# One projection for queries, keys and values in a four-layer attention kernel, and reworked joints between its layers

## The chip, the cores and the metric

The kernel runs on one core of one Trainium2 chip, as one program. The metric is the device time of an execution in microseconds (us). Three runs of the kernel before took 2574.44, 2575.98 and 2577.28 us; their median is 2575.98.

## The reference

Four layers follow one another on a residual of 2048 tokens by 640 features: A, B, A, B. Both A layers share their weights, and so do both B layers.

```
x = A_x
x = x + _A_ref(_layernorm(x), A_wq, A_wk, A_wv, A_wo, A_beta)
x = x + _B_ref(_layernorm(x), B_mem0, B_Wq, B_Wk, B_Wv, B_Wo, B_seg_len)
x = x + _A_ref(_layernorm(x), ...)
x = x + _B_ref(_layernorm(x), ...)
```

Layer A has 32 heads of 20 features and cuts the tokens into 4 segments of 512. In each segment it computes a causal softmax attention within the segment, and reads a memory that the earlier segments have written:

```
q, k, v = x @ wq, x @ wk, x @ wv                  # per head, per segment
a_dot = softmax(q k^T / sqrt(20) + causal mask) v
a_mem = phi(q) M / (phi(q) z + 1e-6)              # phi(t) = t + 1 where t > 0, else exp(t)
o     = g * a_mem + (1 - g) * a_dot               # g = sigmoid(beta), one a head
M, z  = M + phi(k)^T v, z + sum of phi(k)         # after the segment
```

Layer B has 32 heads of 128 features and is recurrent: 64 steps of 32 tokens, each with 8 memory tokens in front that come out of the step before. Its first 8 outputs are the next step's memory.

## The kernel before, in words

**Engines' order.** The tensor engine's instructions (PE) are issued in the order of the program text. In layer A the other engines are ordered by `KeyOrder`: an operation is noted with a due time, the time of its slot (`K.base`) plus a lag by its kind from the table `A_LAGS`, and each engine runs its operations in order of due time. In layer B all engines follow the program text (`_OrdNC`). DMAs are issued from SP's queue.

**Layer A.** `layer_A` works on 32 groups: 4 segments (n) by 8 groups of four heads (G), g = 8n + G. Four heads of 20 features are padded to 32 each and fill 128 rows. A group has four slots, numbered 4g to 4g + 3. In each slot PE first makes "visits": score tiles S (`s_mask` puts the causal mask into PSUM with a whole-array matmul, `s_mm` adds q k^T on 32-row tiles, VectorE takes the row maximum into `a_nm`) and turned tiles T of the group before (`t_round`, exponential on ScalarE into `a_PT`, diagonal cut by GpSimd). After the visits `filler` runs the slot's items, listed in `SLOTS`:

- QP (`proj_q`): the next group's queries, already turned (features on rows, 512 tokens on columns), five matmuls 512 wide; ScalarE copies them to `a_qT`. From the second segment on phi(q) is made from it (`a_EQ`, `a_rq`, `a_phiq`).
- KV0, KV1 (`proj_kv`): keys and values in natural layout (tokens on rows), ten matmuls 160 wide each; ScalarE copies keys to `a_Kn` and values to `a_vaug`, padded to 32 a head.
- KT (`k_turn`): four transposes of the keys and a copy to `a_kT`.
- Q2 (`q_with_max`): the queries go once more through PE with an identity, and the negated row maximum (written by `negmax_rows` in two bf16 parts into columns 20 and 21 of the tile `a_NM`) is turned and added into the same PSUM tile; the copy is `a_q2`, which the T tiles use, so that their scores come out with the maximum taken off.
- UP (`state_up`): phi(k)^T v of the group before, four 128x128 matmuls; VectorE masks the block diagonal (`a_upm`), GpSimd adds it to the state `MZ32` and casts it to `MZb`.
- NUM (`state_num`), PV (`pv`, `norm`), otps, YP0 and YP1 (`out_stage_a`, `out_stage_b`): the memory's read, the attention's output, and the output projection of the segment before with the residual.

The items' PSUM tiles share a pool of two banks (`pg`), so an item waits until the copy of the tile two before it is done. S and T tiles share three tiles of two banks (`psx`). The next segment's layernorm and turn (`seg_load`, `seg_norm`, `seg_tr`) stand in the slots of groups 0 to 4 of a segment (`TPS`).

**Joints.** At the start of a layer A four x tiles are loaded, normalised (`seg_norm`) and turned (`seg_tr`), with idle matmuls (`unread`) between. The first A layer loads plain weights and casts them into padded tiles `a_wq_pad` and `a_wkv` (`load_A_weights`); `keep_padded` stores these to DRAM, and the second A layer loads them from there on SP's queue. `build_gates` makes g and 1 - g after the first visits. At the end of a layer A `out_stage_b` runs for four token tiles: it loads the residual (`a_xr`) for the last two only when it reaches them, and casts each result to bf16 on ScalarE in one single buffer (`a_xnb`) before it is stored; layer B loads that again for its own layernorm.

**Layer B's last step.** Each of the 64 steps projects the next step's tokens (`thin_mm`: b_Ka, b_Qa, b_Kb, b_Qb, 20 matmuls each on four 32-column tiles), where only the 8 memory columns come from the step before. The last step has no next tokens, so its columns (`HXz`) hold the memory alone, and its queries are those of the memory tokens, whose outputs nobody reads. Outputs for the last 8 tokens of four steps are gathered in `OTdef` and projected in four chunks (`od_chunk`, `od_begin`, `od_end`) within later steps; for the last four steps this stands after the last step.

Of the kernel before, what the change touches and what calls it, by code (L numbers as in the profile page):

```python
# [28 lines left out]
D = 640  # L29
NCH = 5  # L30
# [7 lines left out]
def alloc_consts(tc, ctx):  # L38
# [7 lines left out]
    C.pad = cp.tile([128, 2, 12], BF16, name="c_pad")  # L46
# [10 lines left out]
def build_consts(nc, tc, C):  # L57
    with ExitStack() as tctx:
# [13 lines left out]
        for i in range(2):  # L72
            nc.vector.tensor_copy(C.negu[:, i, :], neguf[:])
# [125 lines left out]
class AWeights:  # L199
# [3 lines left out]
A_LAGS = {"dsel": 0.5, "EK": -1.0, "EKm": 1.05, "EQ": 2.0, "Kn": 0.5, "MZ": 3.5, "MZb": 3.5, "NM1": -0.3, "On": 3.2, "adn":  # L203
# [6 lines left out]
def build_gates(nc, pool, W, A_beta):  # L210
    bb = pool.tile([128, 32], BF16, name="a_beta_bf")
    with nc.allow_non_contiguous_dma(reason="beta bcast"):
        nc.sync.dma_start(bb[:], A_beta.partition_broadcast(128))
    e = pool.tile([128, 32], F32, name="a_beta_e")
# [9 lines left out]
def load_A_weights(nc, W, A_wq, A_wk, A_wv, A_wo, padded, stage):  # L224

    first = not padded
    if first:
        for nm, src in (("wq", A_wq), ("wk", A_wk), ("wv", A_wv)):
            nc.sync.dma_start(stage[nm], src.rearrange("(c p) n -> p c n", p=128))
    else:  # L230
        nc.sync.dma_start(W.wq[:].rearrange("p c h s -> p (c h s)"), padded["wq"])
        nc.sync.dma_start(W.wkv[:].rearrange("p c g n -> p (c g n)"), padded["wkv"])
    nc.sync.dma_start(W.wo[:], A_wo.rearrange("(c p) n -> p c n", p=128))
    if first:
        K = yield
        nc.gpsimd.memset(W.wq[:, :, :, 20:32], 0.0)
        cast = K("cast").vector
        cast.tensor_copy(W.wq[:, :, :, 0:20], stage["wq"].rearrange("p c (h d) -> p c h d", d=20))
        for i, nm in enumerate(("wk", "wv")):
            cast.tensor_copy(W.wkv[:, :, :, 80 * i:80 * i + 80], stage[nm].rearrange("p c (g n) -> p c g n", n=80))  # L240
        yield


def keep_padded(nc, tc, W, padded):
    for nm, pad, n in (("wq", W.wq, 1024), ("wkv", W.wkv, 1280)):
        padded[nm] = tc.dram_tile([128, NCH * n], BF16, name=f"a_{nm}_home")
        nc.sync.dma_start(padded[nm], pad[:].rearrange("p c h s -> p (c h s)"))


def layer_A(nc, tc, C, W, x_src, x_dst, src_is_bf16, nseg=4, out_bf16=False, xb_dst=None, load_w=None, side_loads=None):  # L250
# [7 lines left out]
    with ExitStack() as ctx:  # L258
# [4 lines left out]
        W.wq = pw.tile([128, NCH, 32, 32], BF16, name="a_wq_pad")  # L263
        W.wkv = pw.tile([128, NCH, 8, 160], BF16, name="a_wkv")
# [6 lines left out]
        qp3 = pool("a_q3", 3)  # L271
# [18 lines left out]
        MZ32 = ste.tile([128, 8, 128], F32, name="a_MZ32")  # L290
        nc.vector.memset(MZ32[:], 0.0)
        MZb = stm.tile([128, 8, 128], BF16, name="a_MZb")
        vaug = [stm.tile([128, 4, 4, 32], BF16, name=f"a_vaug{i}") for i in range(4)]
        Kn = [stm.tile([128, 4, 4, 32], BF16, name=f"a_Kn{i}") for i in range(2)]
        phik = [ste.tile([128, 4, 4, 32], BF16, name=f"a_phik{i}") for i in range(2)]
        NM = [stm.tile([128, 4, 4, 32], BF16, name=f"a_NM{i}") for i in range(2)]

        def pads(i, eng):
            for on, dst, k in ((i < 2, Kn, 0), (True, vaug, 1)):
                if on:  # L300
                    src = C.pad[:, k, :].unsqueeze(1).unsqueeze(1).to_broadcast([128, 4, 4, 12])
                    (eng.copy if eng is nc.scalar else eng.tensor_copy)(dst[i][:, :, :, 20:32], src)

        nc.vector.tensor_scalar(out=MZ32[:].rearrange("p g (j e) -> p g j e", e=32)[:, :, :, 20],
                                in0=C.identb[:].rearrange("p (j e) -> p j e", e=32)[:, :, 20].unsqueeze(1).to_broadcast([128, 8, 4]),
                                scalar1=1e-6, scalar2=None, op0=ALU.mult)
# [20 lines left out]
        def seg_norm(n_, tt):  # L327
# [4 lines left out]
            for i in range(2):  # L332
                K("st").vector.bn_stats(out=stats[:, i, :], in_=xt[:, 320 * i:320 * i + 320])
# [31 lines left out]
        def out_stage_b(n_, tt, halves=(0, 1)):  # L365
# [3 lines left out]
            if xr is None:  # L369
                xr = wkl.tile([128, D], BF16 if src_is_bf16 else F32, name="a_xr")  # L370
                nc.sync.dma_start(xr[:], x_src[r0:r0 + 128, :])
# [14 lines left out]
            xnb = w1l.tile([128, D], BF16, name="a_xnb")  # L386
            if n_ == nseg - 1:
                nc.scalar.copy(xnb[:], xnew[:])
            else:
                K("xnb").gpsimd.tensor_copy(xnb[:], xnew[:])  # L390
            nc.sync.dma_start(xb_dst[r0:r0 + 128, :], xnb[:])
# [3 lines left out]
        def proj_q(g):  # L395
            n, G = divmod(g, 8)
            s_ = GS[g] = {}
            xnT = SEG[n]["xnT"]
            wqG = W.wq[:, :, 4 * G:4 * G + 4, :].rearrange("p c h s -> p c (h s)")
            QP = pg.tile([128, 512], F32, name="a_QP", tag="pg")  # L400
            for c in range(NCH):
                nc.tensor.matmul(QP[:], lhsT=wqG[:, c, :], rhs=xnT[:, c, :], start=(c == 0), stop=(c == NCH - 1))
            qT = qp3.tile([128, 512], BF16, name="a_qT")
            K("qT").scalar.copy(qT[:], QP[:])
            s_["qT"] = qT
            if n >= 1:
                EQ = w1.tile([128, 512], BF16, name="a_EQ")
                K("EQ").scalar.activation(out=EQ[:], in_=qT[:], func=ACT.Exp)
                rq = w1.tile([128, 512], BF16, name="a_rq")
                K("rq").vector.tensor_scalar(out=rq[:], in0=qT[:], scalar1=0.0, scalar2=None, op0=ALU.max)  # L410
# [3 lines left out]

        def proj_kv(g, hf):
# [973 lines left out]
```

## Time and profile before

| what | us |
|---|---|
| median of three runs | 2575.98 |
| the profiled execution's own time | 2574.74 |
| its span (first to last instruction) | 2573.0 |
| PE busy in the span | 2486.0 |
| DVE (VectorE) busy | 1675.5 |
| ACT (ScalarE) busy | 1519.1 |
| POOL (GpSimd) busy | 696.2 |
| row maxima of A (DVE, 512 instructions) | 395.0 |
| exponentials of A (ACT, 384) | 345.8 |
| k and v projections of A (PE, 1280 matmuls) | 111.2 |
| q projections of A (PE, 320) | 79.9 |
| state updates of A (PE, 192) | 18.6 |

A time is a group's busy time, with overlaps counted once. PE's matmuls overlap in the pipeline, so a mean duration is longer than what one more matmul costs. The profile's page also divides the span into 40 slices of 64.3 us and gives each engine's busy share in tenths; layer A is in slices 1 to 5 and 20 to 25. The chain of waits is followed back from the last instruction: a piece is what the end waited for at that time. In rows of chosen stretches the columns are: length, then busy time (and count) of PE, weight loads (PEld), DVE, ACT and POOL, PE's granted clock, the DMA engines' busy share and GB/s.

### The profile page before, as it was taken

The page shows a single profiled execution, that of the slowest core. Times are in us where ns is not written, and L with a number is a line of the kernel's source. Part 1 is how long each engine was busy: PE and PEld are TensorE (multiplying, and loading weights), DVE is VectorE, ACT ScalarE, POOL GpSimd, SP SyncE. Part 2 cuts the span into 40 slices and gives each one's busy share as a digit, 9 for nine tenths or more (in the row PEclk, how much of TensorE's full clock was granted, in tenths as well). Part 3 has the DMA queues.
Part 4 walks back from the last instruction along what each step waited for, and adds up shares of the span by engine and source line. Part 5 has one row for each costly group of instructions (what it writes and reads, how often), then busy time and mean ns, then how long its engine had stood idle before and what let it go on. Part 6 is the DMA issues. An engine that isn't in the chain of part 4 may idle for free.

```text
span 2573.0 us, 139432 instructions
## 1 busy us (share of the span) xinstructions
PE 2486.0 (97%) x62088; PEld 1639.1 (64%) x62088; DVE 1675.5 (65%) x4597; ACT 1519.1 (59%) x3430; POOL 696.2 (27%) x1471
## 2 busy tenths in 40 slices
PE   7999999999999999999989999999999999999998
PEld 5666576666666666666655665766666666666665
DVE  8999845565556556555579998455655655555555
ACT  6999945555555545444369999445554555555443
POOL 5677621111111111111146776111111111111110
PEclk9999999999999999999999999999999999999999
DMA  4122372222222222121220212721212122111111
GB/s 158 46 85 78 91 239 45 50 48 44 51 45 48 46 50 46 39 39 29 63 84 17 68 53 86 233 47 43 45 41 50 42 45 47 42 42 34 38 26 21
DMA packets 325308, 157.18 MB, mean 61 GB/s; under 512 B 244960, under 2 KB 309600, under 8 KB 322912
## 3 DMA queue, kind: packets, MB, share of 16 engines
q1 hardware_dynamic: 324704, 148.26, 22.1%
q8 instruction: 485, 7.95, 1.3%
q14 instruction: 119, 0.97, 0.1%
HBM read 96.46 MB, written 51.71 MB: 58 GB/s over the span
## 4 chain that ended last, share of the span: by engine, by line
PE 78%; DVE 10%; ACT 8%; issue 2%; DMA 1%; POOL 1%; SPq 0%; ACTq 0%; DVEq 0%; POOLq 0%
PE b_OPS L110 11%; PE b_tail L110 6%; PE b_Ka L110 5%; PE b_Kb L110 5%; PE b_Qa L110 5%; PE b_Qb L110 5%; PE b_Va L110 5%; PE b_Vb L110 4%; DVE a_nm L139 4%; PE b_SP L110 4%; ACT a_PT L139 4%; PE b_vtail L110 3%; PE b_OPSd L110 3%; PE b_OTP L110 3%; PE a_S L110 2%
## 5 line engine op out<-in xcount | busy, mean ns | idle before, releaser
L110 PEld LDWEIGHTS <-b_HX 128*32 128x32 bf16 x15360 | 427.8, 96 | 331.3 <-issue 1.3
L110 POOL TENSOR_TENSOR b_Pn<-b_E,b_rs 128x200 bf16<-128x200 bf16 x128 | 78.0, 609 | 1332.7 <-PE b_Vb L110 1016.9
L139 DVE TENSOR_REDUCE a_nm<-a_S 128x2 f32<-128x512 f32 (+3 forms) x512 | 395.0, 816 | 53.1 <-PE a_S L110 38.1
L139 ACT ACTIVATE a_PT<-a_T 128x1024 bf16<-128x1024 f32 (+1 forms) x384 | 345.8, 904 | 28.3 <-PE a_T L110 21.0
L110 PE MATMUL b_OPS<-b_wo,b_OTsb 128*32 128x320 bf16 x8192 | 303.1, 300 | 1.6 <-issue 0.5
L110 PEld LDWEIGHTS <-b_OTsb 128*32 128x32 bf16 x8192 | 205.7, 96 | 76.3 <-DVE b_OTsb L110 3.3
L139 POOL TENSOR_SCALAR_AFFINE_SELECT a_PT<-a_PT 128x256 bf16<-128x256 bf16 x380 | 188.5, 501 | 154.7 <-ACT a_PT L139 153.4
L110 DVE CAST b_HX<-b_MT 128x8 bf16<-128x8 f32 x372 | 63.6, 172 | 234.0 <-PE b_MT L110 228.3
L110 ACT CAST b_msb<-b_OPS 128x64 bf16<-128x64 f32 x378 | 69.5, 256 | 223.7 <-PE b_OPS L110 223.6
L110 ACT CAST b_kq<-b_Kb 128x512 bf16<-128x512 f32 x128 | 74.9, 585 | 201.4 <-PE b_Kb L110 201.4
L110 DVE COPY b_KT<-b_TPak 128x128 bf16<-128x128 bf16 x128 | 28.7, 224 | 228.2 <-PE b_TPak L110 228.2
L110 DVE TENSOR_SCALAR b_kq<-b_Qa 128x512 bf16<-128x512 f32 x128 | 88.5, 691 | 120.1 <-PE b_Qa L110 116.8
L110 PE MATMUL b_Va<-b_wv,b_HX 128*32 128x512 bf16 x2520 | 161.0, 380 | 0.0
L110 PEld LDWEIGHTS <-b_kq 128*128 128x128 bf16 x2080 | 116.8, 98 | 69.4 <-ACT b_kq L110 56.4
L110 PE MATMUL b_Vb<-b_wv,b_HX 128*32 128x512 bf16 x2520 | 160.7, 379 | 0.0
L110 PE MATMUL b_Ka<-b_wk,b_HX 128*32 128x512 bf16 x2520 | 159.1, 379 | 0.1
L110 PE MATMUL b_Qb<-b_wq,b_HX 128*32 128x512 bf16 x2520 | 158.6, 379 | 0.0
L110 PE MATMUL b_Kb<-b_wk,b_HX 128*32 128x512 bf16 x2520 | 158.6, 379 | 0.0
L110 PE MATMUL b_Qa<-b_wq,b_HX 128*32 128x512 bf16 x2520 | 158.6, 379 | 0.0
L110 DVE CAST b_OTsb<-b_OTP 128x160 bf16<-128x160 f32 (+1 forms) x384 | 130.5, 376 | 38.8 <-PE b_OTP L110 34.6
L110 ACT CAST b_kq<-b_Ka 128x512 bf16<-128x512 f32 x128 | 74.9, 585 | 108.9 <-PE b_Ka L110 108.9
L110 PE MATMUL b_vtail<-b_wv,b_TX 128*32 128x256 bf16 x2880 | 133.9, 271 | 2.4 <-issue 2.3
(206 smaller groups left out, 5432.5 us busy)
## 6 DMA issues: line engine op xcount, KB each, us to landing
b_QKd<-b_tu SPq DMA_DIRECT2D x128, 128.0 KB
b_tl<-b_QKd SPq DMA_DIRECT2D x64, 256.0 KB
b_wv<-in_B_Wv_dram SPq DMA_DIRECT2D x10, 1024.0 KB
b_wo<-in_B_Wo_dram SPq DMA_DIRECT2D x16, 640.0 KB
b_Vth<-b_VTd SPq DMA_DIRECT2D x512, 16.0 KB
b_XO<-xres SPq DMA_DIRECT2D x256, 30.0 KB
b_VTd<-b_vt SPq DMA_DIRECT2D x224, 32.0 KB
b_xt<-xres_bf SPq DMA_DIRECT2D x40, 160.0 KB
```

The lines of the kernel that those rows point to most:

```text
L110: r = f(*a, **k)
L139: r = f(*a, **k)
```

## The change

In layer A the queries are projected with keys and values: one weight tile `W.wqkv` of 240 columns a group (80 of q, 80 of k, 80 of v), two halves of ten matmuls (`proj_qkv`), one copy each into a common tile `QKV` with 12 heads of 32 columns, of which `Qn`, `Kn` and `vaug` are views. `qk_turn` turns keys and queries with eight transposes into one PSUM tile, with one copy. Instead of a second pass with added maxima, `negmax_rows` writes the two parts into columns 20 and 21 of the natural queries, and `q_with_max` turns these once more. The state update runs on four 32-column tiles and takes the block diagonal alone; VectorE adds it to a narrower state and GpSimd spreads and masks it to `MZb`. GpSimd's clamp in `phi_k` works on k itself.

At the joints: constants before the first layernorm, norms and turns interleaved, gates loaded first and made before the first projection; the second A layer's weights come in two pieces, on SP's and ScalarE's queues; the residual tiles of the last segment are loaded with the first turns; the last bf16 copies have a place each. The last step of B leaves out its queries' projections (24 columns of its queries come from the step before, the rest is set to zero), projects its own last 8 tokens in its own output matmuls, and does the remaining chunks before PV; the last stores are split between two queues.

```diff
-A_LAGS = {... "EQ": 2.0, "MZ": 3.5, "phiq": 3.6, "rq": 1.1, ...}
+A_LAGS = {... "EQ": 1.3, "MZ": -0.1, "phiq": 2.1, "rq": 1.2, "q0": 0.0, ...}
...
-        nc.sync.dma_start(W.wq[:].rearrange("p c h s -> p (c h s)"), padded["wq"])
-        nc.sync.dma_start(W.wkv[:].rearrange("p c g n -> p (c g n)"), padded["wkv"])
+        home = padded["wqkv"].rearrange("p (c g n) -> p c g n", c=NCH, g=8)
+        nc.sync.dma_start(W.wqkv[:, :, 0:2, :], home[:, :, 0:2, :])
+        f = nc.scalar.dma_start(W.wqkv[:, :, 2:8, :], home[:, :, 2:8, :])
+        tc.add_manual_dep(f.ins, C.act_last.name, ..., reason="order")
...
-        def proj_q(g):
-            QP = pg.tile([128, 512], F32, name="a_QP", tag="pg")
-            for c in range(NCH):
-                nc.tensor.matmul(QP[:], lhsT=wqG[:, c, :], rhs=xnT[:, c, :], ...)
-            K("qT").scalar.copy(qT[:], QP[:])
+        def proj_qkv(g, hf):
+            if hf == 0 and g >= 4:
+                K("q0").gpsimd.memset(Qn[g % 4][:, :, :, 20:22], 0.0)
+            P_ = pg.tile([128, 2, 240], F32, name="a_QKVp", tag="pg")
+            for t2 in range(2):
+                tt = 2 * hf + t2
+                for c in range(NCH):
+                    nc.tensor.matmul(P_[:, t2, :], lhsT=xnT[:, c, 128 * tt:128 * tt + 128], rhs=W.wqkv[:, c, G, :], ...)
+            K("Kn").scalar.copy(QKV[g % 4][:, 2 * hf:2 * hf + 2, :, 0:20], P_[:]...)
+        def qk_turn(g):
+            T_ = pg.tile([128, 2, 4, 128], BF16, name="a_KQT", tag="pg")
+            for i, src in enumerate((Kn[g % 4], Qn[g % 4])):
+                for tt in range(4):
+                    nc.tensor.transpose(T_[:, i, tt, :], src[:, tt, :, :]..., C.identb[:])
+            K("kT").scalar.copy(kq[:]..., T_[:]...)
...
-                UP = pg.tile([128, 128], F32, name="a_UP", tag="pg")
+                UP = pg.tile([128, 32], F32, name="a_UP", tag="pg")
-                    nc.tensor.matmul(UP[:], lhsT=pk[:, tt, :, :]..., rhs=va[:, tt, :, :]..., ...)
-                K("upm").vector.tensor_tensor(out=upm[:], in0=UP[:], in1=C.bdmask[:], op=ALU.mult)
-                K("MZ").gpsimd.tensor_tensor(out=MZ32[:, G, :], in0=MZ32[:, G, :], in1=upm[:], op=ALU.add)
-                K("MZb").gpsimd.tensor_copy(MZb[:, G, :], MZ32[:, G, :])
+                    for j in range(4):
+                        nc.tensor.matmul(UP[32 * j:32 * j + 32, :], lhsT=pk[:, tt, j, :], rhs=va[:, tt, j, :],
+                                         ..., tile_position=(0, 32 * j), skip_group_check=True)
+                K("MZ").vector.tensor_tensor(out=MZ32[:, G, :], in0=UP[:], in1=MZ32[:, G, :], op=ALU.add)
+                K("MZb").gpsimd.tensor_tensor(out=MZb[:, G, :]..., in0=MZ32[:, G, :]...to_broadcast([128, 4, 32]), in1=C.bdmask[:]..., op=ALU.mult)
...
-            Q2 = pg.tile([128, 512], F32, name="a_Q2", tag="pg")
-            nc.tensor.matmul(Q2[:], lhsT=C.identb[:], rhs=s_["qT"][:], start=True, stop=False, ...)
-            for qc in range(4):
-                nc.tensor.matmul(Q2[:, 128 * qc:128 * qc + 128], lhsT=N_[:, qc, :, :]..., rhs=C.identb[:], ...)
+            Q2 = pg.tile([128, 4, 128], BF16, name="a_Q2", tag="pg")
+            for tt in range(4):
+                nc.tensor.transpose(Q2[:, tt, :], Qn[g % 4][:, tt, :, :]..., C.identb[:])
...
-            K.base = 0.1 * tt - 100.0
+            K.base = 1.2 * tt - 100.0
...
-        SLOTS = (('otps', 'QP', 'UP'), ('Q2', 'KV0', 'NUM'), ('KV1', 'YP0'), ('KT', 'PV', 'YP1'))
+        SLOTS = (('otps', 'QKV0', 'UP'), ('Q2', 'QKV1', 'NUM'), ('KQT', 'YP0'), ('PV', 'YP1'))
...
-                    xr = wkl.tile([128, D], ..., name="a_xr") if tt < 2 else None
+                    xr = wkl.tile([128, D], dt_, name="a_xr") if tt < 2 else wk.tile([128, D], dt_, name="a_xr2", tag="a_no")
...
-            xnb = w1l.tile([128, D], BF16, name="a_xnb")
+                if tt == 0:
+                    d["xnb"] = pon.tile([128, 4, D], BF16, name="a_Onat", tag="Onat")
+                xnb = d["xnb"][:, tt, :]
...
+            if last:
+                nc.gpsimd.memset(QT[s][:, :, 24:32], 0.0)
+            else:
+                Qa = thin_mm(cols, W.wq, 0, "b_Qa")
+                qa = kq(Qa, "dve", SCB)
...
+            if last:
+                od_chunk()
+                oda = dict(od)
+                od_begin(s - 3, XOe, "tail")
+                for _ in range(4):
+                    od_chunk()
...
+            if last:
+                od_end(oda)
+                od_end(nm="e")
...
-        for _ in range(4):
-            od_chunk()
-        od_end()
+        C.act_last = nc._prox["scalar"]._last
```

More of the change, by code (lines that the diff above doesn't have):

```diff
@@ L262, in layer_A @@
         pw = pool("a_w", 1)
[L263 to L264 removed]
+        W.wqkv = pw.tile([128, NCH, 8, 240], BF16, name="a_wqkv")
         pxT = pool("a_xnT", 2)
@@ L609, in norm @@
                 K("On").gpsimd.tensor_tensor(out=Ov, in0=s_["AD"][:, 0], in1=AD[:, 1], op=ALU.add)
+        gates = build_gates(nc, st, W, side_loads[1]) if side_loads is not None else iter(())
+        next(gates, None)
         for tt in range(4):
```

204 lines of the change are left out of this document (92 added, 112 removed), and 4 rows, old and new, of the table A_LAGS.

## The prediction

> **What bounds the kernel now.** I read the page first, then busy time in chosen stretches, then the timeline inside one stretch, then the chain of waits around the places where one layer follows another. Two of the four layers (A) fill slices 1 to 5 and 20 to 25 of the page; there three engines are nearly full at once, while in the B layers only PE is:
>
> ```profile
> PE   7999999999999999999989999999999999999998
> ...
> DVE  8999845565556556555579998455655655555555
> ACT  6999945555555545444369999445554555555443
> ```
>
> So an edit in A pays only where the engine that it relieves ends last. The start of each group's copy of q (ACT, a_qT) marks the groups; in the first A layer from the second on they lie 8.5 to 11.9 us apart. Five of these intervals (columns: us, then busy PE, PEld, DVE, ACT, POOL):
>
> ```profile
> 64.85:73.33 8.48, 8.45 (x126) 5.23 (x124) 7.48 (x13) 7.98 (x15) 5.39 (x14) 1.00 0.10 32
> 109.63:119.74 10.11, 9.10 (x135) 5.83 (x133) 10.01 (x21) 9.45 (x19) 6.76 (x15) 1.00 0.20 64
> 141.80:151.98 10.18, 9.61 (x147) 6.57 (x149) 9.18 (x17) 9.25 (x20) 7.82 (x15) 1.00 0.35 115
> 271.00:279.92 8.92, 8.34 (x124) 5.12 (x122) 7.45 (x13) 8.49 (x16) 5.95 (x12) 1.00 0.09 31
> 289.54:299.72 10.18, 9.53 (x143) 6.42 (x137) 8.73 (x14) 8.89 (x19) 5.93 (x11) 1.00 0.18 55
> ```
>
> The second is led by DVE (10.01 of 10.11): the next segment's layernorms run there, and intervals 1 to 4, 9 to 12 and 17 to 20 of a layer are like it. The other 19 (5 to 8, 13 to 16, 21 to 31) are led by PE, with ACT 0.4 to 1.3 us behind. Inside the first interval:
>
> ```profile
> 64.65 0.39 PE L110 MATMUL a_UP<-a_vaug,a_phik 128*128 128x128 bf16 x4
> ...
> 64.88 0.38 PE L110 MATMUL a_S<-c_negu,c_identb 128*128 128x256 bf16 x2
> ...
> 65.19 0.34 PE L110 MATMUL a_S<-a_kT,a_qT 32*128 32x384 bf16 x2
> ...
> 66.08 0.86 PE L110 MATMUL a_KV<-a_wkv,a_xnT 128*128 128x160 bf16 x10
> ...
> 72.04 1.25 PE L110 MATMUL a_QP<-a_xnT,a_wq_pad 128*128 128x512 bf16 x5
> ```
>
> Matmuls overlap, so the price of one is (length of the run minus one duration) / (count minus one). And the two 256-wide masks take 0.11 each, so the score matmuls on 32-row tiles could start at 65.10; they start at 65.19. A change between whole-array and tiled matmuls costs about 0.09.
>
> The joints, from the chain of waits:
>
> ```profile
> 349.89 3.35 DMA xres_bf<-a_xnb
> ...
> 1277.89 6.15 DMA a_xt<-xres
> ...
> 1291.05 7.21 DMA a_wkv<-a_wkv_home
> 1298.31 2.86 PE a_KV L110 x20
> ...
> 1626.49 4.90 DMA a_xr<-xres
> ...
> 2566.38 2.17 DMA out_dram<-b_xnbd
> ```
>
> Each is time in which a layer waits for a transfer that was issued late: these are what the joint edits aim at.
>
> **The group in A, on PE.** Before: q 5 x 0.217 (from 1.25 and one of 0.380) = 1.09; k and v 20 x 0.069 (0.86, one 0.235) = 1.39; k turned 4 x 0.059 = 0.24; second q 0.23 + 4 x 0.057 = 0.46; state update 4 x 0.057 = 0.23. Sum 3.40. After: 20 matmuls 240 wide. No row is 240 wide; 160 costs 0.069 and 320 (a_YP, five in 0.84, one 0.298) costs 0.136, which bound it; 240 is half way, 0.102, so 2.05 (1.4 to 2.7). Eight turns 0.46, second q four turns 0.23. The state update becomes 16 matmuls on 32-column tiles: 0.10 by B's b_SP (16 in 0.28, one 0.18), 0.17 by their weight loads (16 in 0.17), 0.9 if each cost a whole-array 0.057; I take 0.17, nearest in shape. It now stands between whole-array neighbours, so two mode changes, 0.18, come on top: 0.35 against 0.23. Sum 3.09: PE saves 0.31, and 0.43 in the last segment, which has no update.
>
> The Trainium skill says the same of the mode change ("TensorEngine Tiling (Array Packing)", Key Properties): changing the tiling mode, not merely the tile, drains TensorE. The trace agrees, with the 0.09 above. Without that rule the 48 updates would cost 48 x 0.18 = 9 us less on PE.
>
> **On ACT.** Seven copies become four. In the chain a 512-wide one takes 0.48 when others stand around it, the 160-wide ones 0.18 and 0.21: 3 x 0.48 + 2 x 0.39 = 2.22. Between these rows 0.8 ns an element, so 480 wide costs 0.46, twice; 1024 wide 0.9 (the 1024-wide exponential takes 0.93); second q 0.48. Sum 2.30: ACT gains nothing and loses 0.1 (bounds -0.3 to +0.4). **On DVE** the masked update (128x128, 0.283) goes and the state's addition (128x32) comes: rows of that width take 0.196 to 0.311; I take 0.06 saved (-0.03 to 0.09). **On POOL** addition 0.447, cast 0.296 and clamp 0.452 go; a 128x128 product (0.447), a clamp (0.45) and a memset of 32 elements (0.10 by the small constants, 0.65 by a_phik; I take 0.25) come. Level, and POOL has over 2 us a group to spare.
>
> Bulk, per A layer: 12 PE-led intervals x 0.31 = 3.7; 7 x 0.43 = 3.0; less 0.1 on the seven or so 10.18-us ones, where PE and ACT alternate in the chain, 0.7; 12 DVE-led x 0.06 = 0.7. That is 6.7, **13.4 for both layers** (-6 to +26: below, if ACT's longer copies cost their upper bound in PE-led groups; above, if 240 wide costs nearer 0.08 and three fewer copies remove waits as well).
>
> **Start of the kernel.** Constants move ahead of the layernorm, and norm and turn interleave, so PE could start earlier; but the first projection now needs q, k and v weights cast, and DVE waits until 14.28 for v's. Its cast ends at 15.3, projections take 2.05, copy 0.5, turns 0.46, copy 0.9: first scores near 19.6 against 20.50. The gates' small load goes ahead of SP's x loads (issue 0.7) and may push this back. I take 0.6 saved (-1 to 1.5).
>
> **A to B.** Loading the last two residual tiles early and giving each bf16 copy its own place removes the chain's 3.35 at 349.89 and 4.90 at 1626.49. PE hides most of it under b_tail: its idle there is 1.90 at 354.61, and 1.27 + 0.23 + 0.20 up to 1641. SP's later loads (b_wo at 354.60, behind the delayed stores) move up with it. What comes next are b_Vth's loads (3.76 and 2.79 in the chain), which I leave. I take 3.5 together (1 to 6.5).
>
> **B to A.** The last step of B drops two projections (2 x 1.08) and two turns (0.44); the second key copy is exposed instead (about 0.35). So Vb ends 2.2 earlier, which frees x's buffers: the four x loads are issued near 1274.3 and the last lands near 1281.8 (as 1276.56 to 1284.04). The tail's chunks run before PV, and x_out no longer splits the norms. DVE has 4 x 1.7 of norm, 1.0 of evacuation and 6 x 0.45 of x_out from 1277 on: last xn near 1287, projections from 1287.5, first scores near 1292.5 against 1302.57. The weights: 2.46 MB instead of 2.95, of which the first 0.61 MB go on SP, the rest on ACT's queue behind B's last ACT work; a_wkv moved 1.64 MB in 7.21 us (227 GB/s), so the first piece takes 2.7 to 5.4. I take 9.5 saved (5 to 11.5).
>
> **End.** The softmax chain starts 2.1 earlier, but five chunks of 0.54 fill PE until about 2560; PV, evacuation and 64 b_OPS (2.17) end near 2563. DVE has four od_end operations (0.51 each) before x_out: it ends near 2565.1, against 2569.16 now, where the last one waited 1.39 for a store of the same buffer. The stores after it are the same work on two queues. 4 saved (2 to 5.5).
>
> **Sum:** 13.4 + 0.6 + 3.5 + 9.5 + 4 = 31.0. The profiled execution took 2574.74 (1.74 outside its span of 2573.0) and gives 2543.7; the median of the three runs, 1.24 above it, gives 2545.0. I say **2545**.
>
> **Rivals.**
> *Joints alone pay.* PE's saving goes into waits for ACT, whose two long copies stand between exponentials: bulk 0, 2575.98 - 17.6 = 2558. For it: ACT is 93% busy in the 40 us from 140 on. Against: in 64.85 to 73.33 PE is 8.45 of 8.48. 0.20.
> *More than the sum.* Fewer copies mean one PSUM tile fewer a group (KV1, KT and QP become two halves and one turn); idle like NUM's wait for a_q (11.0 us in all) and the 0.3 to 0.6 PE idle of the 10.18-us intervals go as well: bulk 26, with the joints' better ends 2529. 0.20.
> *Weights late.* If a projection waits for the whole weight tile, or the pieces share the rate, A's second start is at 1291 to 1292: 4 us lost, 2549. For it: one transfer already ran at 227 GB/s with nothing beside it on SP. 0.05. The Trainium skill ("Trainium Kernel Development and Optimization", Key Constraints) has it that DMAs issued from SP and ACT share the same 16 engines, so two queues bring issue time, not rate; no run shown has ACT's queue in use.
> *Slower.* q now passes three hops (copy, turn with k, copy of 1024) before the next group's scores, where it passed one. If ACT runs over a quarter of a group behind at the turn (the slack is one slot of four), the 0.9 copy lies open before the scores: 62 x 0.9 = 56, 2545 + 56 = 2601. It outweighs all savings from 0.5 a group on. For it: ACT in order, its exponentials 0.9 each. Against: the turn is issued a slot earlier than k's was. 0.09.
> That the weights' cut or the moved stores change nothing is in the first rival's neighbourhood: 0.03 within 0.2%.
>
> My forecast itself, 2535 to 2553, has 0.43. Together: faster by over 0.2% 0.88, within 0.2% (about 5 us, what a measurement here can tell from no change) 0.03, slower 0.09. The range of 2518 to 2566 reaches over the joint-only and the larger case; about 0.1 lies above, 0.08 below.
>
> **What would show it.** 240-wide matmuls near 0.10 apart; 16 updates with gaps of 0.09 on both sides; the three kinds of PE-led intervals near 8.2, 9.9 and 8.5, DVE-led ones unchanged; ACT's 480- and 1024-wide copies at 0.46 and 0.9 pitch; the second A layer's first scores some 24 us after the last B step's first projection, where it is 34 now (1268.16 to 1302.57); no ACT wait before a_xnb. I am wrong if intervals lengthen with PE waiting for the copy of the turned q and k, or if PE-led intervals fall by over 0.6.

## The result, and the profile after

The changed kernel takes 2616.69 us (median of four runs, 2612.94 to 2618.96) against 2575.93 for the kernel before (median of four): a ratio of 1.0157, 95% interval 1.0139 to 1.0175. It is 41 us slower where 31 us faster was forecast. Its profiled execution took 2615.74 us, with a span of 2613.8.

The page of the changed kernel, busy tenths in the 40 slices, has the first difference in its last row here, the granted clock of PE. Before, that row is 9 in every slice:

```profile
PE   7899989999999999999989999899999999999999
...
DVE  7899854565555555555578998555655565555555
ACT  5899854555555555544468998445555555554443
...
PEclk8899989999999999999998999899999999999999
```

The five slices with an 8 (1, 2, 6, 22 and 26) lie in the A layers or at their ends, where layer B begins. The trace's record of the granted clock knows two values, 1.00 and 0.50. The stretches at 0.50 last 3.41 us or a multiple of it, but for the last one, which reaches past the end of the span; the expectations below call 3.41 us at half clock a window. Summed up, the time at half clock is 14 us before and 115 us after.

Marks in the trace cut the span at the same events in both kernels: the first row maximum of an A layer, its last PV, the first b_tail after it, the first b_Ka of B's step 0 and of its step 63. All in us, first and second layer:

| stretch | before | after | forecast change, both |
|---|---|---|---|
| start to first row maximum | 20.8 | 22.3 | -0.6 |
| bulk of A, to the last PV | 316.9, 317.1 | 337.2, 335.9 | -13.4 |
| last PV to first b_tail | 7.9, 7.9 | 18.4, 18.4 | -3.5 for this row and the next |
| first b_tail to step 0 | 37.7, 36.6 | 34.1, 34.1 | |
| step 0 to step 63 | 884.7, 886.6 | 882.1, 883.3 | 0 |
| step 63 to A's first maximum | 34.9 | 30.0 | -9.5 |
| last step 63 to the end | 22.0 | 18.2 | -4 |

So the bulk costs 39 us and the two joints from A to B 15 us net; from B to A and at the end the kernel is faster. The stretch from step 0 to step 63 is edited nowhere, and over the profiles of all fifteen kernels it takes 882.1 to 886.9: a difference of a few us between two single profiles can be chance.

**The bulk.** What PE waits for in the whole changed kernel (columns: total us, times, longest):

```profile
PE a_T L110 <- ACT a_PT L139: 29.9, 56, 1.0
PE b_lntps L110 <- DVE b_xt L110: 18.4, 4, 7.6
```

Before, PE waited 4.2 us for a_PT, the exponentials that free the PSUM tiles of T. And ACT itself now waits for the turn:

```profile
ACT a_kqT L139 <- PE a_KQT L110: 30.6, 62, 1.5
```

Both are seen in one group. ACT (start, length, what; in brackets idle before and its releaser):

```profile
86.73 0.58 ACT L139 CAST a_QKV<-a_QKVp 128x480 bf16<-128x480 f32 x1
87.91 1.01 ACT L139 COPY a_kqT<-a_KQT 128x1024 bf16<-128x1024 bf16 x1 [0.60 <-PE a_KQT L110]
88.82 2.44 ACT L139 ACTIVATE a_PT<-a_T 128x1024 bf16<-128x1024 f32 x3
```

and PE in the same microseconds:

```profile
86.91 0.39 PE L110 MATMUL a_T<-a_q,a_kqT 32*128 32x512 bf16 x2
87.23 0.64 PE L110 MATMUL a_KQT<-c_identb,a_QKV 128*128 128x128 bf16 x8
...
88.67 0.39 PE L110 MATMUL a_T<-a_q,a_kqT 32*128 32x128 bf16 x4 [0.26 <-DVE a_nm L139]
89.90 0.28 PE L110 MATMUL a_T<-a_q,a_kqT 32*128 32x256 bf16 x2 [0.83 <-ACT a_PT L139]
90.12 1.20 PE L110 MATMUL a_PV<-a_QKV,a_PT 128*128 128x32 bf16 x40
...
92.43 2.07 PE L110 MATMUL a_QKVp<-a_wqkv,a_xnT 128*128 128x240 bf16 x10
```

The T of slot 2 is done at 87.30 (86.91 + 0.39) and its exponential could start. But ACT's next instruction is the copy of the turn, whose matmuls end at 87.87. ACT stands 0.60, copies for 0.9, and only then, at 88.82, makes the exponential. PE's third T of this stretch needs that PSUM tile: it stands 0.83, until 89.90. Each engine waits for the other, in 56 and 62 of the 64 groups. The T and its exponential belong to the group before the slot's own, the copy to the group after it; neither needs the other, and only ACT's order ties them together.

The stretch has a second price. Stretches of 3.41 us around it (columns: length, busy time of PE, weight loads, DVE, ACT and POOL, PE's clock, DMA share, GB/s):

```profile
84.00:87.43 3.43, 3.43 (x55) 2.03 (x40) 2.60 (x7) 2.93 (x5) 1.07 (x3) 1.00 0.00 0
87.43:90.84 3.41, 2.32 (x49) 1.45 (x48) 2.39 (x4) 2.93 (x4) 1.22 (x4) 1.00 0.15 47
90.84:94.25 3.41, 3.41 (x38) 2.10 (x34) 2.74 (x3) 2.24 (x4) 3.33 (x8) 0.50 0.31 112
```

PE is busy for 2.32 of 3.41 in the second row, much of it with tiles of 32 rows, and the next stretch runs at half clock: its ten projection matmuls take 2.07 where ten at full clock take 1.20. The Trainium skill ("TensorE: Matmul & The Clock Gate", "A second HAM failure mode: psum-queue depth-cycling") tells of a kernel whose short idle times between matmul groups, from cycling through PSUM, made the clock swing between half and full. This trace agrees: no wait of PE inside the bulk is listed as longer than 1.0 us, and of the 115 us at half clock 82 lie there.

**From A to B.** SP's queue in the changed kernel:

```profile
363.66 0.34 SPq L380 DMA_DIRECT2D xres<-a_xnew  x1
...
368.73 0.32 SPq L391 DMA_DIRECT2D xres_bf<-a_Onat  x1
369.49 0.65 SPq L847 DMA_DIRECT2D b_xt<-xres_bf  x1
```

The first loads for B's layernorm (b_xt) stand behind A's last eight stores. Before, they were issued at 329.81, ahead of these. PE then waits 7.6 us at B's first turn (b_lntps, above).

### The profile page after: what moved, and what is told of

Its sections match the earlier page's. It is cut to its first block, busy times and chain, and to the rows that moved or that the text cites. A ratio compares the mean times of both kernels' runs of the same rounds, so it can differ in the third digit from the quotient of the medians.

```text
span 2613.8 us, 140012 instructions
## 1 busy us (share of the span) xinstructions
PE 2498.6 (96%) x62440; PEld 1655.1 (63%) x62440; DVE 1684.0 (64%) x4593; ACT 1526.9 (58%) x3238; POOL 707.8 (27%) x1484
## 4 chain that ended last, share of the span: by engine, by line
PE 82%; ACT 9%; DVE 6%; issue 1%; DMA 1%; POOL 1%; SPq 0%; ACTq 0%; DVEq 0%; POOLq 0%
PE b_OPS L110 11%; PE b_tail L110 6%; PE b_Ka L110 5%; PE b_Kb L110 5%; PE b_Qb L110 5%; PE b_Qa L110 5%; PE b_Va L110 5%; PE b_Vb L110 4%; ACT a_PT L139 4%; PE b_SP L110 4%; PE a_S L110 3%; PE b_vtail L110 3%; PE b_OPSd L110 3%; PE a_QKVp L110 3%; PE b_OTP L110 3%; ACT a_kqT L139 2%
## 5 line engine op out<-in xcount | busy, mean ns | idle before, releaser
L139 ACT ACTIVATE a_PT<-a_T 128x1024 bf16<-128x1024 f32 (+1 forms) x384 | 328.9, 894 | 23.0 <-PE a_T L110 17.5
L110 PE MATMUL a_T<-a_q,a_kqT 32*128 32x512 bf16 (+3 forms) x1024 | 133.1, 310 | 44.4 <-ACT a_PT L139 29.9
L110 PE MATMUL a_QKVp<-a_wqkv,a_xnT 128*128 128x240 bf16 x1280 | 169.5, 286 | 3.9 <-DVE a_wqkv L139 2.5
```

The source lines that it names most:

```text
L110: r = f(*a, **k)
L139: r = f(*a, **k)
```

## The experiments

Five theories. **1**: the changed group uses the array less in two of its four slots, and the clock falls with it. **2**: the smaller A tiles shift the others, so that b_xt's buffers lie over tiles that A frees last, and the loads are ordered behind the stores. **3**: from B to A, DVE stands at a statistics instruction of A ahead of B's last copies. **4**: in before no engine alone sets a group. **5** came after the first eight runs: the place of ACT's copy in ACT's order. Times below are medians; ratios are to the kernel before measured beside each run (2580.6 to 2581.8 us), which takes out that it ran some 5 us slower there than at first. Stretches, waits and half clock are compared with the first profile of the kernel before, which does not take it out: its clock is 0.998, that of the later runs of the same kernel 0.994 to 0.997, about 0.0025 x 2575 = 6 us (an estimate).

**e1 and e2: the change cut in two.** The group of one kernel with the joints of the other.

> This is the kernel before with the group of the changed kernel (joint projection, the turn of keys and queries, the 32-wide state update, the slots and lags), but with the joints, the start and the end of before. Theory 1 and 2 (the group lowers the array's use in two of its four slots, and the clock with it; and its smaller tiles let the first loads of B's layernorm lie over tiles that A frees last): the bulk of both A layers costs some 39 us and the two A to B joints some 10 us each, and the 4.9 and 3.9 us that the changed kernel saves from B to A and at the end are missing: 2635 us (2625 to 2645), some 25 to 30 windows at half clock, the first B layernorm loads issued behind A's last stores. Rival (the joint edits make the A to B joint late): 2610 to 2618, loads issued ahead of the last stores as in before.

> The kernel before with the group of before and all other edits of the changed kernel (start, A to B, B to A, end). Theory: the bulk of A is as in before (clock 0.998, 4 to 6 windows at half clock), B to A saves 5, the end 4, A to B between 0 and 10 in all: 2562 us (2553 to 2568). Rival (these edits themselves cost the 7 to 8 us that each A to B joint grew by): 2580 to 2585.

Measured: e1 2631.9 us, ratio 1.0191 (1.0175 to 1.0207); e2 2566.1 us, ratio 0.9934 (0.9918 to 0.9951). Both as theory 1 and 2 expect. With the group alone the bulk is 336.9 and 337.4 and last PV to b_tail 22.4 and 22.9; with the joints alone 316.9 and 319.0, and 9.2 and 9.3. So the group carries the whole loss, that of the A to B joint too. The surprise is from B to A: 28.2 with the group alone and 34.7 with the joint edits alone, against 34.9, where e2 was to save 5. The weights' load tells why. Before, it is issued 23.1 us after the first b_Ka of step 63, and PE waits 4.3 for it at the first a_KV. In e2 it is issued at 22.1, on ACT's queue, and PE waits 2.8. In e1 the loads of `W.wqkv` are issued from 10.4 on, and PE does not wait for them.

**e3: b_xt's buffers over tiles that are free early.**

```diff
+        w1 = pool("a_wk1", 1)
+        pool("a_room", 1).tile([128, 768], BF16, name="a_room")
         qp4 = pool("a_q4", 4)
...
-        w1 = pool("a_wk1", 1)
...
+        bx = pool("b_x", 1)
         hp = pool("b_hx", 3)
         tx = pool("b_tx", 2)
-        bx = pool("b_x", 1)
```

> The changed kernel with three pools moved (the buffers of EQ and rq ahead of those of the turned queries and keys, 1.5 KB of room, and B's input buffers first among B's small pools), so that the four buffers into which B's first layernorm loads go lie over tiles that A has finished with a segment earlier. Nothing that is computed changes. Theory 2: the four loads are issued ahead of A's last stores, last PV to first B tail falls from 18.4 to 8 to 10 us in both joints: 2598 us (2593 to 2604). Rival (what holds the joint is the half clock and the tail's evacuations, not the loads): less than 5 us saved, 2612 to 2618.

Measured: 2597.2 us, ratio 1.0057 (1.0040 to 1.0074). The loads now stand ahead of the stores:

```profile
351.81 0.65 SPq L848 DMA_DIRECT2D b_xt<-xres_bf  x1
...
354.75 0.58 SPq L846 DMA_DIRECT2D b_xt<-xres_bf  x1
...
361.87 0.34 SPq L381 DMA_DIRECT2D xres<-a_xnew  x1
```

Last PV to b_tail falls from 18.4 to 9.2 in both joints, the span by 18.3 us; the bulk stays. Theory 2 is shown: pools in another place, no instruction changed.

**e4 and e6: the second projection a slot later.** First the projection and the turn alone, then (on e3) NUM as well.

```diff
-        SLOTS = (('otps', 'QKV0', 'UP'), ('Q2', 'QKV1', 'NUM'), ('KQT', 'YP0'), ('PV', 'YP1'))
+        SLOTS = (('otps', 'QKV0', 'UP'), ('Q2', 'NUM'), ('QKV1', 'YP0'), ('KQT', 'PV', 'YP1'))        # e4
+        SLOTS = (('otps', 'QKV0', 'UP'), ('Q2', 'PHI'), ('QKV1', 'NUM', 'YP0'), ('KQT', 'PV', 'YP1'))  # e6
```

> The changed kernel with its second joint projection of a group moved from slot 1 to slot 2 and the turn of keys and queries from slot 2 to slot 3; same instructions. Theory 1 (the clock follows the array's use, and the changed kernel has both projections in slots 0 and 1 and none in 2 and 3): under 12 windows at half clock, mean clock over 0.99, the bulk of both A layers 20 to 40 us shorter: 2590 us (2575 to 2600). Rival (the bulk is lost to the longer path from projection by the turn and its 1024-wide copy to the scores, which is now a slot shorter of time): the wait for the copy of turned keys and queries grows, 2617 to 2650, whatever the clock does.

> The kernel of e3 (2597 us) with the second joint projection moved to slot 2 and the turn to slot 3, as in e4, and NUM moved from slot 1 to slot 2 as well, since e4 lost 38 us in segments 1 and 2 with PE waiting 102.6 us at NUM for phiq, which comes behind the turn. Theory: what e4 gained in segment 0 (6.9 and 5.5 us) stays and segments 1 to 3 get the clock back too: 2570 us (2560 to 2582), at most 12 windows at half clock. Rival (any later turn is exposed, at phiq or at the scores): 2597 to 2640.

Measured: e4 2695.9 us, ratio 1.0438 (1.0418 to 1.0457); e6 2639.1 us, ratio 1.0224 (1.0206 to 1.0242). Both miss what theory 1 expected; e6 lies in its rival's range, e4 46 us above its own. In segment 0, which has no NUM, the groups get faster (6.9 and 5.5 us in e4). Later each order meets another wait. In e4 it is PE's for phiq, made from the turned queries:

```profile
PE a_NUM L110 <- DVE a_phiq L139: 102.6, 48, 2.9
```

In e6 it is DVE's, standing at a residual addition whose YP comes later in slot 2:

```profile
DVE a_xr L139 <- PE a_YP L110: 37.3, 22, 2.9
```

A slot's items can't be moved without their lags: the other engines' places are set by the same table.

**e5: more array use in slots 2 and 3.** On e3, four more matmuls a group that nothing reads.

```diff
             PV = pg.tile([128, 4, 4, 32], F32, name="a_PV", tag="pg")
+            for _ in range(2):
+                nc.tensor.matmul(PV[:, 0:2]..., lhsT=C.identb[:], rhs=C.negu[:]..., start=True, stop=True, ...)
...
+            for _ in range(2 if r + pr == 0 else 0):        # in t_round, ahead of T
+                nc.tensor.matmul(Y[:, 0, 0:256], lhsT=C.identb[:], rhs=C.negu[:]..., start=True, stop=True, ...)
```

> The kernel of e3 (2597 us) with four more full-array matmuls a group that nothing reads: two of 256 columns ahead of the first T of slot 2, two ahead of PV in slot 3; some 0.43 us of PE time a group, 28 us over 64 groups. Theory 1 (the lost time of the bulk is the half clock, which follows stretches with little use of the array): at most 8 windows at half clock, the bulk of each A layer 13 to 20 us shorter in spite of the added work: 2563 us (2553 to 2575). Rival (PE's time, or the waits for ACT, set the group): the added matmuls cost up to 28 us, 2597 to 2625.

Measured: 2629.9 us, ratio 1.0186 (1.0169 to 1.0203), above even the rival's range. The time at half clock does fall, from 90 to 55 us in the profiles; but the bulk grows from 335.7 and 335.5 to 351.7 and 350.7. The waits say why:

```profile
PE a_T L110 <- ACT a_PT L139: 55.9, 56, 1.2
```

```profile
ACT a_kqT L139 <- PE a_KQT L110: 65.3, 62, 2.0
```

Both have doubled from e3's 29.4 and 30.1: the filler stands ahead of the turn, so ACT waits longer at its copy, and PE longer for the exponential behind it. Less half clock and a longer time: the half clock alone, theory 1, does not give the loss. This run led to theory 5.

**e9: ACT's copy one place later.** On e3, one number. The due time of the copy is its slot, 2, plus 0.3 plus the lag: 2.4, where slot 2's exponential is due at 2.5 and slot 3's first at 3.2.

```diff
-          ... "kT": 0.1, ...
+          ... "kT": 0.3, ...
```

> The kernel of e3 (2597 us, ratio 1.0057 to 1.0061 with before) with one number changed: the place of ACT's 1024-wide copy of the turned keys and queries in ACT's order, from ahead of the exponential of slot 2's T to just behind it. Theory 5 (that copy makes ACT stand 0.5 us a group at the turn, 30.1 us in all, while the exponentials behind it hold the buffers that PE's next T waits for, 29.4 us in all, and the stretch in which PE waits is the one that halves the clock): both waits fall under 10 us, the bulk of each A layer gets 12 to 22 us shorter, fewer than 14 windows at half clock: 2560 us (2550 to 2573). Rival (the half clock comes from the group's smaller use of the array alone): the waits go, the windows stay at 20 or more, and the time falls by less than 12 us: 2585 to 2597.

Measured: **2544.5 us**, ratio 0.9862 (0.9846 to 0.9879), better than theory 5's range, and faster than both kernels. ACT and PE in a group of segment 0:

```profile
70.92 1.02 ACT L139 ACTIVATE a_PT<-a_T 128x1024 bf16<-128x1024 f32 x1
71.84 1.01 ACT L139 COPY a_kqT<-a_KQT 128x1024 bf16<-128x1024 bf16 x1
72.73 1.53 ACT L139 ACTIVATE a_PT<-a_T 128x1024 bf16<-128x1024 f32 x2
```

```profile
70.43 0.39 PE L110 MATMUL a_T<-a_q,a_kqT 32*128 32x512 bf16 x2
70.75 0.64 PE L110 MATMUL a_KQT<-c_identb,a_QKV 128*128 128x128 bf16 x8
...
71.99 0.50 PE L110 MATMUL a_T<-a_q,a_kqT 32*128 32x128 bf16 x6
72.42 1.16 PE L110 MATMUL a_PV<-a_QKV,a_PT 128*128 128x32 bf16 x40
...
74.64 1.20 PE L110 MATMUL a_QKVp<-a_wqkv,a_xnT 128*128 128x240 bf16 x10
```

No bracket is left in these rows: the exponential fills the time in which ACT stood, the T matmuls that stood apart run as one group of six, and the next projections run at full clock. Over the kernel:

```profile
PE a_T L110 <- ACT a_PT L139: 0.2, 1, 0.2
```

```profile
ACT a_kqT L139 <- PE a_KQT L110: 1.7, 3, 0.6
```

At the scores PE waits 5.8 us more for exponentials, where it was 2.4 in e3. The bulk is 308.8 and 309.7, the time at half clock 23 us, in the bulk 10 where e3 has 78. The two prices can be set against each other, as an estimate: PE's idle time in both bulks falls from 62 to 40 us, and 68 us less at half clock are 34 us of full-speed work, together 57, where the bulk got 53 shorter. For the changed group theory 5 is shown: one number takes away both waits and nearly all the half clock in the bulk.

**e12: that number alone**, without e3's pools.

> The changed kernel (2616.7 us, ratio 1.0157) with the one number of e9 changed and the tiles left where they were, so the first loads of B's layernorm stay behind A's last stores. If the two causes are independent: as much less as e9 is below e3 (1.0059 to 0.9862), a ratio of 0.996, 2566 us (2559 to 2573), last PV to first tail still near 18 us. Rival (the copy's place also made the joint late, or the gain needs the moved tiles): over 2580, or under 2552.

Measured: 2564.1 us, ratio 0.9930 (0.9913 to 0.9946). The bulk is 310.3 and 311.0, the joints keep their 18.7 and 19.5. In medians the number is worth 52.6 us here and 52.7 on e3, as independent causes would give; by the ratios, where 0.996 was expected, it is 0.003 more. So the two causes add up to within some 8 us, and together they are more than the loss.

**e13: the same place in the kernel before**, whose copy of the turned keys is 512 wide.

```diff
-          ... "kT": 0.1, ...
+          ... "kT": -0.2, ...
```

> The kernel before with one number changed: ACT's 512-wide copy of the turned keys goes from behind the first exponential of slot 3 to ahead of it. Theory 5 (a copy that waits for a late turn, placed in front of an exponential whose buffer PE needs, makes ACT and PE wait for each other, and the clock falls in the stretch where PE waits, whatever the group's mix): PE waits 0.2 to 0.6 us a group more for exponentials or at the scores, 10 to 40 us more: 2600 us (2586 to 2620), and more than 8 windows at half clock. Rival (it takes the changed group's smaller use of the array and its 1024-wide copy): within 10 us of before, the windows as in before.

Measured: 2589.1 us, ratio 1.0031 (1.0020 to 1.0042): the rival's side. ACT does stand at the copy:

```profile
ACT a_kT L139 <- PE a_KT L110: 26.1, 49, 0.9
```

Before, that row is 0.8. But PE's waits for exponentials, at T and at the scores, grow only from 4.2 to 14.7 us (29.9 and 2.5 in the changed kernel). The half clock grows little: the runs have clocks of 0.992 to 0.995, those of the kernel before beside them 0.995 and 0.996. So the place costs something in this group too, 8 us, but theory 5's size, and that it halves the clock whatever the group's mix, falls. What the changed group adds to it, the slot, the copy of 0.9 or the smaller use of the array, was not taken apart.

**e10: POOL's maximum earlier.** On e9, `"EKm": 1.05` becomes -0.8.

> The kernel of e9 with one more number changed: POOL's maximum of the keys with zero, for which DVE waits 17.2 us in all in e3, 1.85 slots earlier in POOL's order. Theory (that wait lies on DVE's path to the next scores' maxima): 3 to 8 us less than e9. Rival (DVE has the time back elsewhere, and POOL's masks of the exponentials are now later): between 2 us less and 6 us more than e9.

Measured: 2546.3 us, ratio 0.9869 (0.9851 to 0.9887), no difference from e9, in the rival's range. But it does not test the theory: DVE's wait of 17.2 us in e3 no longer stands among e9's waits, so moving ACT's copy had already taken it away, and e10 had nothing left to take.

**e8 and e11: what sets a group in before.** Work left out of the kernel before: two of five matmuls of each query projection; then the feature map of the queries.

```diff
-            for c in range(NCH):
+            for c in range(3):                # e8, proj_q
...
-                EQ, rq, phiq ...; s_["phiq"] = phiq
+                s_["phiq"] = qT               # e11
```

> The kernel before with two of the five matmuls of each query projection left out (128x512, some 0.215 us each), so that the queries are a sum over three fifths of the inputs: 0.43 us of PE time less a group and nothing else changed. What the prediction assumed (PE sets the time of a group): 0.43 x 64 = 27 us less than before, ratio 0.9895. Theory 4 (in before PE, DVE and ACT are all 90 to 93 per cent busy in a group, so PE's work is not what sets it, and what PE is relieved of lowers the array's use and the clock): ratio 0.998 to 1.01, with more than 4 windows at half clock.

> The kernel before with the positive feature map of the queries left out (no exponential, no maximum and no sum of them: the queries themselves go to NUM), in the 48 groups that use it: ACT 0.71 us, DVE some 1.0 us less a group, PE's work unchanged. Theory 4 (in before no engine alone sets a group; e8 took 0.43 us a group from PE and the bulk of a layer fell by under 1 us): 0.1 to 0.35 us a group, 5 to 17 us less than before, ratio 0.9935 to 0.998, and no more than half of what was taken. Rival (PE alone sets it): within 3 us of before.

Measured: e8 2570.5 us, ratio 0.9958 (0.9946 to 0.9969): 10 us, between the 27 of PE's share and theory 4, which said at most 5. e11 2561.2 us, ratio 0.9925 (0.9907 to 0.9942): 19 us, above theory 4's 5 to 17, and less than half of what was taken. The profiles show e8's gain group by group. Of the five intervals in the prediction these are the counterparts of the first, fourth and third in e8, by the same marks:

```profile
66.49:74.61 8.12, 8.12 (x123) 5.18 (x120) 7.47 (x13) 7.92 (x16) 5.48 (x13) 1.00 0.11 34
270.09:278.78 8.69, 8.16 (x122) 5.08 (x120) 7.65 (x13) 8.38 (x17) 5.96 (x11) 1.00 0.11 32
142.09:152.27 10.18, 9.48 (x147) 6.37 (x139) 9.31 (x17) 9.25 (x20) 7.85 (x15) 1.00 0.37 119
```

The group of 8.48, in which PE was busy for 8.45, falls by 0.36 when PE is relieved of 0.43: there PE does set the time, as the prediction said. The group of 8.92 falls by 0.23, and by 0.41 in e11 (8.51): neither engine alone sets it. The group of 10.18 stays at 10.18 in both, although PE was busy for 9.61 of it, and the DVE-led one of 10.11 at 10.10 in e8. Over the 28 intervals of each layer from the fourth on e8 gains 6 us, where 0.43 each would be 24. So theory 4 holds for most groups, not for all. Its half clock is not shown: e8's profile has 21 us, 10 of them in the bulk, where the profile of before has 14 and none, but the clocks of e8's runs (0.995 to 0.997) are those of the kernel before beside them.

What sets the group of 10.18 stands in its chain of waits, which goes through ACT:

```profile
148.03 0.49 ACT a_kT L139
148.52 0.04 issue
148.56 0.84 PE a_YP L110 x5
```

Its other pieces on ACT are the copies a_qT (0.48), a_q (0.49) and a_oT (0.69) and three exponentials; neither a_QP nor the feature map is in it.

**e7: DVE's order from B to A.** On e3, order edges: the copies b_OTsb ahead of the statistics of A's second input tile, B's additions behind A's first normalised tile.

```diff
+                elif not src_is_bf16 and n_ + i == 0 and tt == 1:
+                    tc.add_manual_dep(f.ins, C.ot_last.name, K.info, reason="order")
...
+            if not src_is_bf16 and n_ + tt == 0:
+                tc.add_manual_dep(C.xo_ins, f.ins.name, K.info, reason="order")
```

> The kernel of e3 (2597 us) with three order edges on DVE at the B to A joint: B's last copies of the turned attention output ahead of the statistics of A's second input tile, and B's last additions behind A's first normalized tile. Theory 3 (PE's 4.3 us idle at the last output projection is DVE standing at a statistics instruction that waits for its load): that idle falls under 2.5 us and the first A scores come 2 to 5 us earlier: 2593 us (2590 to 2596). Rival (the first scores are set by the loads of A's input whatever DVE does first): B to A unchanged within 1 us, 2596 to 2599.

Measured: 2596.7 us, ratio 1.0061 (1.0042 to 1.0080), as e3. PE in e3, then in e7:

```profile
1299.65 0.46 PE L110 MATMUL b_OPS<-b_wo,b_OTsb 128*32 128x320 bf16 x8 [3.60 <-DVE b_OTsb L110]
...
1305.91 0.83 PE L110 MATMUL a_W<-c_negu,c_identb 128*128 128x256 bf16 x6 [1.59 <-DVE b_XO L110]
```

```profile
1296.00 2.36 PE L110 MATMUL b_OPS<-b_wo,b_OTsb 128*32 128x320 bf16 x64 [1.75 <-DVE b_OTsb L110]
1302.31 1.46 PE L110 MATMUL a_W<-c_negu,c_identb 128*128 128x256 bf16 x6 [3.95 <-DVE b_XO L110]
```

The wait is cut as expected and comes back one step later: B to A takes 28.6 against 29.0, and the kernels that are alike in this stretch lie between 27.9 and 31.4. Theory 3 had the wait right and its worth wrong. In e7 the chain to the first scores goes through DVE, where A's statistics and B's additions follow one another from 1294.40, when a load of A's input has landed, to 1302.27.

## Why the prediction was wrong

**The step that failed** is "ACT gains nothing and loses 0.1". Its durations hold (the 1024-wide copy has a pitch of 0.89 where 0.9 was said; ACT's busy time in segments 1 and 2 is 149.4 before and 149.6 in e9). What it left out is the place: a wait put at nothing. The turn moved from slot 3 to slot 2, its lag stayed at 0.1, and so the copy was moved past slot 2's exponential in ACT's queue. The prediction gave the move as a mark in favour ("the turn is issued a slot earlier than k's was") and never asked what now stands behind it. Its slower rival knew the copy and ACT's order, and 56 us was near the size (e3's span less e9's is 56.8), but it had the copy open before the next scores, with ACT a quarter of a group late. In the trace the copy lies open before an exponential of the group before, ACT is not late but stands waiting, and the price is waits of both engines and half clock. That 62 x 0.9 comes near is luck. The sign that the prediction named, PE waiting for the copy of the turned q and k, did not show either: at the scores PE waits for it 1.8 us in all.

**The clock** was in no step. Half of 115 us is 58 us of full-speed work, against 7 before; with the copy in its place and e3's pools (e9) it is 11.

**Bulk.** With only the copy's place mended (e12) the bulk falls by 12.7 us for both layers, with e3's pools (e9) by 15.5, against 13.4 forecast. The sum comes near by luck: its terms miss in both directions. 240-wide matmuls are 0.102 apart (20 in 2.21, one 0.27), as forecast, and the changes of tile are there: in e9 the first update starts 0.196 after the last projection matmul, and the next matmul 0.11 after the last update. But in the intervals that PE did set (e8), PE lost 0.2 and the interval only 0.06, from 8.48:

```profile
65.69:74.12 8.43, 8.26 (x134) 5.30 (x137) 7.43 (x12) 7.98 (x13) 5.31 (x13) 1.00 0.10 33
```

The 8.92 ones fell to 8.30 and the 10.18 ones to 9.58, 0.62 and 0.60 where 0.43 and 0.21 were said. "The other 19 are led by PE" was read from shares, and against a line that the prediction shows: in its fourth interval ACT has 8.49 and PE 8.34. In the groups of 10.18 the chain goes through four of ACT's copies; in e9, where they take 9.58, it goes through PE and DVE and has no piece on ACT. So the copies taken off ACT seem to have been worth something there that "ACT gains nothing" left out; this is read from the chains and was not tried. In segments 1 and 2 a group of e9 has 0.19 less on PE and 0.22 less on DVE (0.06 was forecast). On POOL the clamp was given 0.45 and took 1.01:

```profile
L139 POOL TENSOR_SCALAR a_rk<-a_QKV x48: 1007/1011/1012, 24.2 to 1566.4; 128x320 bf16<-128x320 bf16 x48
```

What it costs in time was not tried (e10 does not show it).

**A to B.** The edits themselves are worth what was said or more: with the joints alone (e2) last PV to step 0 falls from 45.6 and 44.5 to 43.1 and 42.1, 4.9 against 3.5. What failed is that a smaller tile was counted as nothing but smaller. It moved every later pool, and B's first loads with them: 18.3 us (e3).

**B to A.** 4.9 in place of 9.5, below its range. PE's early end was right: b_Vb ends 2.15 earlier, and A's x loads are issued from 6.6 to 8.0 us after the first b_Ka of step 63, where 6.3 was said. The step that failed is DVE's: the last xn was to end 19 us after that mark and ends at 23.1, 22.4 before, behind statistics that wait for their loads and among B's additions; to mend one piece of that order gave nothing (e7). What was gained came with the weights: the joint edits alone gave 0.2 (e2), the new group 6.7 (e1), with PE's wait for its weights gone.

**Start and end.** The start was 0.6 to be saved, is 1.5 longer, and lies between 20.5 and 22.3 in the changed kernel, e3, e7, e9 and e10, which start alike: nothing can be said of it. The end saved 3.85 against 4.

With both causes gone, e9 is 36 us faster than the kernel before beside it (2544.5 against 2580.6), where the sum said 31 for the changed kernel. That is a kernel with another copy's place and other pools, and the terms above miss, so it does not make the forecast right; it says that these two places, neither an instruction more or less, turn the gain into a loss.

## What to carry to other kernels

When an item moves to another slot, write down for each in-order engine which instructions its parts now stand in front of, and whether what these feed is needed before the item's own input can be ready; a duration on an engine with time to spare says nothing of this. In a stretch in which several engines are over 90% busy the busiest need not set the time: read the chain of waits there, or leave out some work of one engine and see which groups get shorter. Look for a wait of two engines on each other before looking for work to remove. When tiles change size, compare where every later tile lies and in which order the transfers are issued.

## What the runs showed of the hardware

A PE that is busy for 68% of 3.41 us (2.32 of it, much in 32-row tiles) was followed by a stretch at half clock. The Trainium skill ("TensorE: Matmul & The Clock Gate", Part 1: The HAM clock gate) names an idle window of about 3.4 us as what brings half clock. In this bulk no stretch is idle, so here partly busy ones were enough. Cut into stretches of 3.41 us in step with the clock's record, both bulks of the changed kernel have 171 at full clock. In the 24 that are followed by half clock PE is busy for 0.49 to 0.79 of the time, and a whole-array matmul is under way for 0.23 to 0.45; in the 147 others it is at least 0.69 and 0.40. The ranges overlap, and before has a stretch of 0.63 and 0.37 that half clock does not follow, so no border comes out of these traces.

The mean over a layer does not set the clock. From e3 to e5 PE's busy share of the bulk goes from 0.91 to 0.89 and the share with a whole-array matmul under way stays at 0.68, yet the half clock in the bulk falls from 78 to 44 us: e5 adds whole-array matmuls where a group has few. What a single stretch must hold was not tried.
